# Batch 5's q and k loads between two parts of batch 4's value loads, and its crossbar transfers one tile later, in an attention and feed-forward kernel

## The chip, the cores and the metric

The kernel runs on one core of a Trainium2 chip. The metric is the time of one execution on the device in microseconds (us), the median of several runs. A profiled execution gives, besides, a trace of every instruction on each engine: TensorE (PE, and PEld for its weight loads), VectorE (DVE), ScalarE (ACT), GpSimd (POOL), SyncE (SP). GpSimd and SyncE do little here but issue transfers, each in its own order, on two queues that the same 16 DMA engines serve.

## The reference

Two things are computed one after the other, and only the last result is stored.

```python
# attention, (batch, heads, seq, head_dim) = (8, 8, 576, 64)
scores = scale * np.matmul(q, k.transpose(0, 1, 3, 2))
rel = pos[:, None] - pos[None, :]
mask_plain = (rel >= 0) & (rel < window)                                  # window = 32, heads 0 to 3
mask_dil = (rel >= 0) & (rel < window * dilation) & (rel % dilation == 0)  # dilation = 4, heads 4 to 7
scores = np.where(masks[None, :, :, :], scores, -1000000000.0)
attn = softmax(scores);  attn_out = np.matmul(attn, v)
# feed-forward over the 8 * 576 = 4608 tokens, d_model 512, d_ff 2048
h = np.maximum(x @ w_in, 0.0)
out = (h * h @ w_out).astype(np.float32)
```

Softmax is written short here. The inputs are float32 in memory; the loads turn them into bfloat16.

## The kernel before, in words

**Feed-forward.** The tokens are worked on in tiles: four of 256 and then seven of 512 (`ffn_groups`). Each tile is a list of groups. A group of layer one multiplies four k-slices of the weights with the attention result in `xT` (L888), ScalarE applies the relu and writes `h2T` (L901), VectorE squares it (L902). A group of layer two is four matmuls of L930; after four of them the sum is copied out by ScalarE (L936) and stored by SyncE (L857). A tile of 512 has 16 groups of layer one and 16 of layer two. All tiles together make one list of 288 groups, numbered from 0; a tile of 512 tokens has 32 (`G`). Tile 2 is groups 64 to 95, tile 3 groups 96 to 127, tile 4 groups 128 to 159.

**Attention in between.** Batches of attention are laid between the groups of tiles ahead of those that use their result. From batch 3 on (`NATURAL`) this goes by numbered steps: a list `steps` of (group, priority, batch, code), sorted, and taken off after each group. The codes are
- `R`, `K`, `Q` (`arrange`, L471 to L482): VectorE copies transposed q and k from the buffer `xx` to where the matmuls want them (`qT`, `kbd`). `R` takes the ends of each sequence, and `R00` begins with the second part of q and of k.
- `V` (`quadrants`, L617): a visit of TensorE, which computes scores of some pairs of heads and the weighted sums of others. A pair is two heads; each batch has four, 0 to 3.
- `E` (L654, L656, L663): ScalarE takes the exponentials of the scores, VectorE multiplies them by the mask, and for pairs 0 and 1 adds two sums.
- `L`, `X` (L630 to L645): the normalisation, by ScalarE and then VectorE, into `xT`.

For batch b a base `t = G * (b - 1)` fixes the groups: 96 for batch 4, 128 for batch 5. Batch 4 has a visit after group 111 that takes the weighted sum of its pair 0, and one after group 119 that takes scores of batch 5's pairs 2 and 0. Batches from `PAIRED` = 5 on copy `K` and `Q` for pair 0 and pair 1 at separate times.

**Transfers.** `load_qk` (L171) loads one part of q and of k of a batch on GpSimd's queue to a staging buffer, `qb` and `kb` (three of each, chosen by `STAGE`). Part 0 is 64 rows, part 1 is 80 rows, 256 elements of each head in a row. `load_v_rows` loads v on the same queue: with `d` the rows for the dilated heads and two blocks (L444, L449, eight transfers), with `0` and `1` the plain heads of that pair in sixteen-row pieces (L457, eight transfers each). A GpSimd transfer is issued only when the one eight places before it has landed. `cross_all` issues four crossbar transfers of a batch on SyncE's queue (L238, `DMA_TRANSPOSE`): k and q of part 0, then k and q of part 1, from the staging buffer to `xx[b % 2]`. They share SyncE's queue with the stores, in the order of the program.

**What sets the order.** Everything is issued in the order in which the program runs: the loop at L1128 goes through the groups, and after each group runs the codes that `PROGRAM` has at that place (its `|` separates groups), then the steps that are due. `Lb:q0...` and `Lb:q1...` are q and k loads of batch b, part 0 or 1; `Lb:V` with letters are its value loads; `Lb:x` its crossbar transfers. In `PROGRAM` batch 5 has its loads at groups 76 and 77, the values of batch 4 follow at 78, `L5:x` comes at 84, batch 6's loads at 93 and 94, and batch 5's values at 95. The later batches have theirs by `LOAD_V`, `CROSS` and `LOAD_QK` (L1055 to L1057). An engine takes an instruction only after the one before it, so the group at which something stands fixes its place in the queue and not the time at which it runs.

Of the kernel before, what the change touches and what calls it, by code (L numbers as in the profile page):

```python
# [26 lines left out]
    "| | | | | | | | | m n | | | | | | 1q1 1q3 | 1q2f 1k2f | 1k1a 1v3 | 1a2 | 1v2 1k0a 1q0v | 1o2 | 1a0 1a1 | 1k3 "  # L27
    "1o0 1o1f | 1a3 1Q0 | 1K0 1o3 | 1Q1 1K1 | 1Q2 | 1b0 | | 1Q3 1K2 L2:vwp L3:q00123 L3:q10123 L2:vwdr | L2:x | | "
    "2q0 | | 2k0 1V2 | 1b2 1p0 | 1b1 1V3 1K3 | L3:x | 1p2 1p1f | 2a0 1b3 | 2k1l 2b0 2o0 1p3f 2k1h | 2q1 | | 2p0 "
    "L3:Vd0 L4:q00123 L4:q10123 L3:V1 2a1 | 2b1 | | 2o1 | | | 2p1f | | | | L4:x | | | | | | | | | | | | | | | | "  # L30
    "L5:q10123 | L5:q00123 | L4:V | | | | | | L5:x | | | | | | | | | L6:q00123 | L6:q10123 | L5:V"
)


# [29 lines left out]
def kernel(  # L64
# [11 lines left out]
    B, H, S, D = q.shape  # L76
# [20 lines left out]
    PAIRED = 5  # L97
# [339 lines left out]
    def load_v_rows(b: int, which="d01"):  # L437


        if "d" in which:  # L440
            vds[b] = vd_pool.tile([P, NE // 2, 2, RES * D], bf16, name="vd")
            for hl, rows in enumerate(sides):
                for e in range(NE // 2):
                    nc.gpsimd.dma_start(  # L444
                        vds[b][rows, e, :, :],
                        v[b, H // 2 + 2 * e + hl, 0:512, :].rearrange("(m p r) d -> p m (r d)", p=64, r=RES),
                    )
                for i in (0, 8):
                    nc.gpsimd.dma_start(  # L449
                        v_rows[b % 2][rows, NE // 2 :, i, :],  # L450
                        v[b, H // 2 + hl : H : 2, 64 * i : 64 * i + 64, :].rearrange("h p d -> p h d"),
                    )
        for e in (int(x) for x in which if x != "d"):
            for hl in range(2):
                p0 = sides[hl ^ crossed(b, e)].start
                for r in range(RES):
                    nc.gpsimd.dma_start(  # L457
                        v_rows[b % 2][p0 + 16 * r : p0 + 16 * r + 16, e, :, :],
                        v[b, 2 * e + hl, :, :].rearrange("(i m r) d -> r m i d", r=RES, m=16)[r],
                    )  # L460
# [591 lines left out]
    G = 2 * NF  # L1052
# [1 line left out]

    LOAD_V = {b: G * (b - 2) for b in range(6, B)}  # L1055
    CROSS = {b: G * (b - 1) - 48 for b in range(6, B)}
    LOAD_QK = {b: G * (b - 3) - 10 for b in range(7, B)}  # L1057
    groups, steps = [], []
    for tk0, nt in [(NT // 2 * t, NT // 2) for t in range(4)] + [(NT * t, NT) for t in range(2, NTILES)]:
        groups += ffn_groups(tk0, nt)  # L1060
# [8 lines left out]
    for b in range(NATURAL, B):  # L1069
        t = G * (b - 1)  # L1070
        early = b == NATURAL
        def visit(at, scs, pvs):
            steps.append((at, 2, b, "V0" + "/".join(",".join(f"{x}{y}" for x, y in z) for z in (scs, pvs))))

        def expo(e, *at):
            steps.extend((y, 1, b, f"E{e}{x}") for x, y in enumerate(at))

        def norm(e, at):
            steps.extend([(at, 3, b, f"L{e}"), (at + 1, 0, b, f"X{e}")])

        after = b + 1 < B
        if b < PAIRED:
            start = 59 if early else t - 8
            second = t + (7 if early else 5)
            x = 3 if early else 0
            if early:
                visit(start, [(b, 2)], [(XB, 2), (XB, 3)])
                for e in (2, 3):
                    steps.extend([(start + e - 2, 3, XB, f"L{e}"), (start + e - 1, 0, XB, f"X{e}")])
            expo(2, *((start + 4, start + 7) if early else (start + 7, start + 9)))  # L1090
            visit(second, [(b, x)], [(b, 2)])
            norm(2, second)
            expo(x, second + 3, second + 5)
        if early:
            visit(t + 17, [(b, 0), (b, 1)], [(b, 3)])
            expo(0, t + 18, t + 18)
            expo(1, t + 18, t + 18)
            norm(3, t + 18)
            visit(t + 24, [(b + 1, 2)], [(b, 0), (b, 1)])
            norm(0, t + 24)  # L1100
            norm(1, t + 25)
        else:
            visit(t + 15, [(b, 3), (b, 1)], [(b, 0), (b, 2)][: 1 + (b >= PAIRED)])
            steps.extend((t + 15, 3, b, f"E1{x}") for x in range(2))
            if b >= PAIRED:
                norm(2, t + 15)
            expo(3, t + 16, t + 16)
            norm(0, t + 17)
            visit(t + 23, [(b + 1, 2), (b + 1, 0)] if after else [], [(b, 1), (b, 3)])
            if after:  # L1110
                steps.extend((t + 23, 3, b + 1, f"E0{x}") for x in range(2))
                steps.extend((t + 27 + 2 * x, 1, b + 1, f"E2{x}") for x in range(2))
            norm(3, t + 23)
            norm(1, t + 24)
        at = t - 14 if b < PAIRED else t - 26
        for x, code in enumerate(("R00", "R01", "R10", "R11")):
            steps.append(((57, 57, 54, 55)[x] if early else at + x, 1, b, code))
        for x, code in enumerate(("K00", "K01", "K10", "K11", "Q00", "Q01", "Q10", "Q11")):
            if b < PAIRED:
                steps.append((t + x if early else t - 6 + x, 1, b, code))  # L1120
            else:
                steps.append((t - 23 + x - max(x - 4, 0) // 2, 1, b, code + "0"))
                steps.append((t - 8 + x, 1, b, code + "1"))
    steps.sort(key=lambda x: x[:2])
    program = [x.split() for x in PROGRAM.split("|")]
# [2 lines left out]
    for g, group in enumerate(groups):  # L1128
        for b in [x for x in CROSS if CROSS[x] == g]:
            cross_all(b)  # L1130
        for b in [x for x in LOAD_V if LOAD_V[x] == g]:
            load_v_rows(b)
        for b in [x for x in LOAD_QK if LOAD_QK[x] == g]:
            for part in range(2):
# [36 lines left out]
```

## Time and profile before

| | us |
|---|---|
| median of three runs | 302.16 |
| the three runs | 301.69, 302.16, 302.79 |
| the profiled execution | 301.41 |
| its span, from first to last instruction | 299.6 |

| queue | packets | MB | share of 16 engines |
|---|---|---|---|
| GpSimd's (software) | 49280 | 18.43 | 56.0% |
| SyncE's (hardware) | 33120 | 16.18 | 25.9% |

The granted TensorE clock was 1.000 over the span. The profile's page gives, for each engine, its busy time; a row of 40 slices with the busy share in tenths; the chain of work that ended last, followed back from the end; and the groups of instructions by source line. The trace can be asked for more: instructions in order of time (start, length, engine, line, output and input, and in brackets the idle time before it with what ended that), who waited for whom, and for a stretch of time what each DMA queue moved (packets, MB, share) and how long transfers took from issue to landing. The tiles can be placed by the chain: tile 2's layer one starts at 88.57 us, its layer two at 103.15, tile 3's layer one at 119.05, its layer two at 135.11, tile 4's layer one at 150.02.

### The profile page before, as it was taken

How to read it: one execution, taken by the hardware profiler on the slowest of the kernel's cores; microseconds unless marked ns; L12 is line 12 of the kernel's file. 1: busy time of each engine (PE TensorE's matmuls, PEld its weight loads, DVE VectorE, ACT ScalarE, POOL GpSimd, SP SyncE). 2: the span in 40 equal slices, each digit the busy share in tenths (PEclk: the TensorE clock that was granted, in tenths of full speed). 3: DMA queues.
4: the chain of work that ended last, by engine and by line, in shares of the span. 5: the costliest groups of instructions: out<-in, count | busy, mean ns of one | idle time of the engine just before them, and what ended most of it. 6: DMA issues, size and time to landing. Idle time of an engine off the chain costs nothing.

```text
span 299.6 us, 7596 instructions
## 1 busy us (share of the span) xinstructions
PE 289.8 (97%) x3016; PEld 168.2 (56%) x3045; DVE 165.9 (55%) x495; ACT 193.7 (65%) x405; POOL 130.5 (44%) x210
## 2 busy tenths in 40 slices
PE   8889999999999999999999999999999999999994
PEld 3579756968855455554455455545555455445443
DVE  2675556998858654696748574856455235004300
ACT  7787658859967765786667666767666566126411
POOL 8589872585884538849838389000000000000000
PEclk9999999999999999999999999999999999999999
DMA  7999999999999999999994997012101200121022
GB/s 111 200 169 214 206 153 226 186 161 199 187 121 192 158 192 162 190 149 145 184 213 30 132 187 80 4 29 70 48 0 27 83 35 0 37 71 35 0 72 70
DMA packets 83123, 35.42 MB, mean 118 GB/s; under 512 B 52624, under 2 KB 78480, under 8 KB 83088
## 3 DMA queue, kind: packets, MB, share of 16 engines
q0 software_dynamic: 49280, 18.43, 56.0%
q1 hardware_dynamic: 33120, 16.18, 25.9%
q8 instruction: 24, 0.39, 0.5%
q10 hardware_dynamic: 688, 0.33, 0.5%
q14 instruction: 11, 0.09, 0.1%
HBM read 37.40 MB, written 9.44 MB: 156 GB/s over the span
## 4 chain that ended last, share of the span: by engine, by line
PE 90%; DMA 5%; POOL 1%; issue 1%; ACT 1%; DVE 0%; ACTq 0%; POOLq 0%
PE pf L930 41%; PE pf L888 41%; DMA w_in<-in_moe_w_in_dram 3%; DMA kb<-in_k_dram 2%; PE po L617 2%; PE pa L258 1%; PE pf L617 1%; PE pa L617 1%; PE pd L617 1%; POOL qb L171 1%; PE pa L332 1%; PE po L395 1%; PE pd L397 0%; POOL kb L171 0%; POOL vbd L219 0%
## 5 line engine op out<-in xcount | busy, mean ns | idle before, releaser
L888 PE MATMUL pf<-xT,w_in 128*128 128x512 bf16 (+1 forms) x697 | 128.3, 340 | 1.9 <-DMA w_in<-in_moe_w_in_dram 1.5
L930 PE MATMUL pf<-w_out_sb,h2T 128*128 128x512 bf16 (+2 forms) x570 | 127.4, 373 | 1.5 <-issue 0.6
L888 PEld LDWEIGHTS <-w_in 128*128 128x128 bf16 x704 | 77.7, 113 | 47.9 <-DMA w_in<-in_moe_w_in_dram 1.6
L901 ACT ACTIVATE h2T<-pf 128x512 bf16<-128x512 f32 x144 | 83.7, 599 | 30.0 <-PE pf L888 29.7
L902 DVE TENSOR_TENSOR h2T<-h2T 128x512 bf16<-128x512 bf16 x144 | 60.4, 424 | 60.9 <-ACT h2T L901 58.8
L930 PEld LDWEIGHTS <-h2T 128*128 128x128 bf16 x592 | 55.4, 98 | 61.1
L936 ACT COPY osb<-pf 128x512 f32<-128x512 f32 (+1 forms) x36 | 20.7, 574 | 52.6 <-PE pf L930 49.5
L457 POOL DMA_DIRECT2D vbd<-in_v_dram x80 | 43.9, 558 | 7.8 <-DMA vbd<-in_v_dram 2.9
L444 POOL DMA_DIRECT2D vd<-in_v_dram x20 | 12.1, 612 | 14.9 <-PE pf L617 6.1
L449 POOL DMA_DIRECT2D vbd<-in_v_dram x20 | 11.9, 606 | 12.1 <-DMA qb<-in_q_dram 5.4
L640 ACT ACTIVATE rec<-rec 128x576 f32<-128x576 f32 x22 | 15.0, 683 | 0.6
L192 POOL DMA_DIRECT2D vbd<-in_v_dram x16 | 10.9, 686 | 9.9 <-DMA kb<-in_k_dram 3.6
L654 ACT ACTIVATE pt<-pa 128x384 bf16<-128x384 f32 (+1 forms) x26 | 11.8, 497 | 4.5 <-DVE xT L645 2.7
L171 POOL DMA_DIRECT2D qb<-in_q_dram x18 | 13.2, 736 | 1.5 <-POOLq L1155 0.8
L643 DVE TENSOR_TENSOR xT<-po,rec 128x512 bf16<-128x512 f32 x13 | 9.0, 692 | 8.3 <-ACT rec L640 8.0
L171 POOL DMA_DIRECT2D kb<-in_k_dram x18 | 13.1, 730 | 0.7 <-DMA kb<-in_k_dram 0.7
L656 DVE TENSOR_TENSOR pt<-pt,mask_n 128x448 bf16<-128x448 bf16 (+1 forms) x20 | 7.1, 372 | 9.9 <-ACT pt L654 9.8
L656 DVE TENSOR_TENSOR pt<-pt,mask_f 128x384 bf16<-128x384 bf16 x24 | 8.2, 354 | 5.8 <-ACT pt L654 5.7
L471 DVE COPY qT<-xx 64x576 bf16<-64x576 bf16 (+1 forms) x32 | 11.1, 346 | 0.7
L643 DVE TENSOR_TENSOR xT<-pf,rec 128x512 bf16<-128x512 f32 x9 | 6.2, 691 | 7.4 <-ACT rec L640 7.3
L617 PEld LDWEIGHTS <-vbd 64*64 64x64 bf16 x248 | 6.8, 107 | 3.8 <-issue 2.9
L473 DVE COPY kbd<-xx 64x320 bf16<-64x320 bf16 (+3 forms) x32 | 8.4, 261 | 0.7
(138 smaller groups left out, 314.4 us busy)
## 6 DMA issues: line engine op xcount, KB each, us to landing
qb<-in_q_dram POOLq DMA_DIRECT2D x7, 320.0 KB, 7.8
kb<-in_k_dram POOLq DMA_DIRECT2D x7, 320.0 KB, 9.3
vd<-in_v_dram POOLq DMA_DIRECT2D x32, 64.0 KB, 7.0
w_in<-in_moe_w_in_dram POOLq DMA_DIRECT2D x4, 512.0 KB, 7.8
w_out_sb<-in_moe_w_out_dram POOLq DMA_DIRECT2D x4, 512.0 KB, 12.2
out_dram<-osb SPq DMA_DIRECT2D x16, 128.0 KB, 5.9
qb<-in_q_dram POOLq DMA_DIRECT2D x7, 256.0 KB, 6.8
kb<-in_k_dram POOLq DMA_DIRECT2D x7, 256.0 KB, 8.5
```

The source lines that it names most:

```text
L171: nc.gpsimd.dma_start(t[0:n, part, hs, :], src[b, hs, t0 : t0 + RES * n, :].rearrange("h (p r) d -> p h (r d)", r=RES))
L444: nc.gpsimd.dma_start(vds[b][rows, e, :, :], v[b, H // 2 + 2 * e + hl, 0:512, :].rearrange("(m p r) d -> p m (r d)", p=64, r=RES),)
L457: nc.gpsimd.dma_start(v_rows[b % 2][p0 + 16 * r : p0 + 16 * r + 16, e, :, :], v[b, 2 * e + hl, :, :].rearrange("(i m r) d -> r m i d", r=R ...
L617: nc.tensor.matmul(out, lhs, rhs, start=begin, stop=True, skip_group_check=True)
L640: nc.scalar.activation(rec[:, :], rec[:, :], ACT.Exp, scale=-1.0)
L643: nc.vector.tensor_tensor(out=tok[:, :, 16:M], in0=byr(o[:, :]), in1=byr(rec[:, 0:512]), op=ALU.mult)
L656: nc.vector.tensor_tensor(out=pt, in0=pt, in1=mask, op=ALU.mult)
L888: nc.tensor.matmul(to, w_in_sb[piece][:, kt, c0 : c0 + 509 : 4], rhs, start=(kt == kts[0] and x == 0), stop=(kt == kts[-1] and x == per - ...
L901: nc.scalar.activation(hv, acc[u][:, :].rearrange("p (x n) -> p x n", x=per), ACT.Relu)
L902: nc.vector.tensor_tensor(out=hv, in0=hv, in1=hv, op=ALU.mult)
L930: nc.tensor.matmul(cur[m][:, c0:c1], h2[:, f, P * m : P * m + P], w_out_sb[:, f, c0:c1], start=(f == 0), stop=(f == NF - 1),)
L936: (nc.vector.tensor_copy if last and part == 1 else nc.scalar.copy)(osb[:, c0:c1], cur[m][:, c0:c1])
```

## The change

Four edits, all in the order of work; no instruction is added or removed.

```diff
@@ PROGRAM
-    "L3:Vd0 L4:q00123 L4:q10123 L3:V1 2a1 | 2b1 | | 2o1 | | | 2p1f | | | | L4:x | | | | | | | | | | | | | | | | "
-    "L5:q10123 | L5:q00123 | L4:V | | | | | | L5:x | | | | | | | | | L6:q00123 | L6:q10123 | L5:V"
+    "L3:Vd0 L4:q00123 L4:q10123 L3:V1 2a1 | 2b1 | | 2o1 | | | 2p1f | | | | L4:x | | | | | | | | | | | | | | | | | "
+    "| L4:Vd0 L5:q00123 L5:q10123 L4:V1 L6:q00123 L6:q10123 | | | | | | | | | | | | | | | | | L5:V | | L5:x"
@@
-    LOAD_QK = {b: G * (b - 3) - 10 for b in range(7, B)}
+    LOAD_QK = {b: G * (b - 3) - 2 for b in range(7, B)}
@@
-        at = t - 14 if b < PAIRED else t - 26
+        at = t - (14, 23, 26)[(b >= PAIRED) + (b > PAIRED)]
@@
-                steps.append((t - 23 + x - max(x - 4, 0) // 2, 1, b, code + "0"))
+                steps.append((t - (20 if b == PAIRED else 23) + x - max(x - 4, 0) // 2, 1, b, code + "0"))
```

On GpSimd's queue, batch 4's values for the dilated heads and the first plain pair now stand ahead of batch 5's q and k, whose part 0 comes before part 1 where it was the other way round; batch 4's second plain pair follows, then batch 6's q and k, then batch 5's values as before. All of these but batch 5's values are handed out after group 78. On SyncE's queue, batch 5's four crossbar transfers move from group 84 to group 97, behind five stores of tile 2. On VectorE, batch 5's `R` copies move from groups 102 to 105 to groups 105 to 108, and the `K` and `Q` copies for its pair 0 from groups 105 to 111 to groups 108 to 114. Batch 7's q and k are handed out at group 126 and not 118, which leaves them at the same place on GpSimd's queue. The instructions of TensorE and ScalarE keep their order.

## The prediction

> **What bounds the kernel now.** I read the shares by engine first, then the chain that ended last, then TensorE's own waits, then the order of work on SyncE's queue and VectorE around the change. The first three say that TensorE sets the time:
>
> ```profile
> PE 289.8 (97%) x3016; PEld 168.2 (56%) x3045; DVE 165.9 (55%) x495; ACT 193.7 (65%) x405; POOL 130.5 (44%) x210
> ...
> DMA  7999999999999999999994997012101200121022
> ...
> PE 90%; DMA 5%; POOL 1%; issue 1%; ACT 1%; DVE 0%; ACTq 0%; POOLq 0%
> ```
>
> TensorE is busy for 289.8 of 299.6 us; of the 9.8 us left, its longest waits by name are 1.5 us for the first weights and 1.1 us at the start, both before 21 us. In the windows 100 to 125 and 125 to 150 us I find 0.3 us of idle and none. So in the stretch that the change touches (95 to 145 us) there is nothing to win on TensorE in this execution, and the change can only matter by putting a wait where none is. The DMA row shows where such a wait could come from: the 16 DMA engines are at nine tenths or more from 7.5 us to 157 us. Any transfer that is moved later there has to share with what is running then.
>
> Now the transfers that are moved. SyncE's queue, with the start and length of each issue:
>
> ```profile
> 89.03 1.37 SPq L238 DMA_TRANSPOSE xx<-kb  x1
> ...
> 97.00 1.29 SPq L238 DMA_TRANSPOSE xx<-qb  x1
> 98.39 11.84 SPq L857 DMA_DIRECT2D out_dram<-osb  x5
> 110.42 1.28 SPq L238 DMA_TRANSPOSE xx<-kb  x1
> 111.81 1.82 SPq L238 DMA_TRANSPOSE xx<-qb  x1
> 113.74 2.27 SPq L238 DMA_TRANSPOSE xx<-kb  x1
> 116.10 2.30 SPq L238 DMA_TRANSPOSE xx<-qb  x1
> 118.50 2.87 SPq L857 DMA_DIRECT2D out_dram<-osb  x5
> 134.55 1.25 SPq L238 DMA_TRANSPOSE xx<-kb  x1
> ```
>
> The sets at 89, 110 and 134 us are those of batches 4, 5 and 6. The one at 110.42 is batch 5's; its last transfer landed 5.2 us after 116.10, at 121.3. VectorE reads it first at 128.90, so it had 7.6 us in hand:
>
> ```profile
> 109.74 0.19 DVE L479 COPY kbd<-xx 64x128 bf16<-64x128 bf16 x1 [1.47 <-DMA xx<-qb]
> ...
> 127.80 0.69 DVE L643 TENSOR_TENSOR xT<-po,rec 128x512 bf16<-128x512 f32 x1
> ...
> 128.90 0.19 DVE L479 COPY kbd<-xx 64x128 bf16<-64x128 bf16 x1
> ...
> 132.33 0.41 DVE L902 TENSOR_TENSOR h2T<-h2T 128x512 bf16<-128x512 bf16 x1
> 132.66 0.34 DVE L656 TENSOR_TENSOR pt<-pt,mask_n 128x384 bf16<-128x384 bf16 x1
> 133.04 0.34 DVE L663 TENSOR_TENSOR kbd<-pt 128x128 bf16<-128x128 bf16 x2
> ...
> 137.22 0.31 DVE L471 COPY qT<-xx 64x576 bf16<-64x576 bf16 x1
> ```
>
> VectorE works without a gap from 127.80 to 140.24. What TensorE needs of it are two things: the masked scores of batch 4's pair 0 (done 133.38) for the visit at 133.85 (after layer-one group 111), and batch 5's rearranged q and k (done 137.53) for the visit at 141.75 (after group 119).
>
> **The change, part by part.** *Loads.* GpSimd's queue has the same instructions in another order. From 95.23 on, eight issues of L444 and L449 (some 0.61 each) and eight of L457 (0.56) now go before batch 5's four loads: 4.9 + 4.5 = 9.4 us, so these start at about 104.6 instead of 95.23. They took 7.1 to 12.4 us to land; four issues of 0.73 bring the last to 107, landing at 114 to 119. That is ahead of the transposes' new place (below), so by itself it costs 0. If the last landed at 121 or later, SyncE would wait by as much, added one for one to what follows. Batch 4's second half of L457 comes after them and is read only at 141.75: 0. Batch 6's loads, which began at 121.06 after all of this, now follow without batch 5's transposes beside them and start at some 113 to 118. Batch 7's loads (now handed out at group 126, before at 118) keep their place between batch 5's and 6's values on GpSimd's queue: 0.
>
> *Transposes.* Four issues on SyncE move behind five stores. The last two of these need the eviction of the fourth token block, 119.09 + 0.59 = 119.68; at 2.87/5 = 0.57 an issue the queue is free at 120.9. So 110.42 becomes 120.9, 10.5 us later, and of the 7.6 us in hand nothing is left unless VectorE's own move helps. The stores themselves go earlier (the first of the five at about 112 instead of 118.5): they free an output buffer that nobody waits for here, 0.
>
> *VectorE.* Its reads of the transposed data move three groups later. Now three squarings (L902, 0.43 each) and one mask (0.41) come before the first read: 128.87 + 1.70 = 130.6. That first read needs the fourth transfer of the set, because it takes the second part of q. Behind it on VectorE stand a squaring, the second mask and its two sums: 0.43 + (133.41 - 132.33 = 1.08) = 1.51 us. TensorE wants these at 133.85. So the last transfer may land at 133.85 - 1.51 = 132.3 at the latest; after that each us costs TensorE one us. The second need: from the first read to the end of the q copies VectorE had 11.34 us of work; without the four instructions that now go ahead, 9.64. With the landing at T, q is ready at T + 9.64, wanted at 141.75 plus whatever the first wait cost; at T = 134.2 that adds 0.2 us. The squarings are wanted later than both: in the new order the q copies come behind the sixteenth of them.
>
> *How long the set takes to land* is the disputed term. From first issue to last landing the six sets of this trace took 9.0 (batch 2), 13.3 (3), 20.7 (4), 10.9 (5), 12.5 (6) and 9.9 us (7). What tells them apart is what the other queue moved meanwhile; in the windows of batch 4's, 5's and 6's sets it was:
>
> ```profile
> q0 software_dynamic: 4899, 1.95, 85.9%
> ...
> q0 software_dynamic: 2838, 0.43, 52.7%
> ...
> q0 software_dynamic: 2907, 0.41, 50.9%
> ```
>
> Packets, MB and share; the transposes' own queue had 4990, 5017 and 4893 packets. So 0.42 MB beside it means 11.7 us, 1.95 MB means 20.7: 5.9 us for each MB. At 120.9 I expect about half of batch 6's loads still running (0.3 of 0.59 MB), then batch 5's value rows (0.13 MB of L444 and most of L457's 0.29): 0.7 MB, 11.7 + 0.28 x 5.9 = 13.3 us, batch 3's own figure. Landing at 134.2. Ends: 9.0 us (129.9, no wait) and 20.7 us (141.6, a wait of 9.3 us). I take 13.3 because the neighbours will be more than batch 5's and 6's sets had and less than half of batch 4's.
>
> The Trainium skill ("DMA: Bandwidth & Descriptors", section "Latency and other measured facts") gives transposes an effective 261 GB/s. A set reads 2 x 8 x 576 x 64 bf16 = 1.18 MB, an estimate of 4.5 us by that page: it would be there before 130.6 and the whole sum would be 0. No set in this trace came under 9.0 us, so I go by the sets.
>
> **Sum.** 134.2 + 1.51 - 133.85 = 1.9, plus 0.2 at the second visit: 2.1 us. The profiled execution took 301.41 us (span 299.6 and 1.8 around it), which gives 303.5. Its time lies below all three timed runs (301.69 to 302.79, median 302.16); the median plus 2.1 is 304.3. Some of that 0.75 may be a wait that the change removes (next part), so I forecast 303.8, some 0.1 below the middle of 303.5 and 304.3.
>
> **Rivals.** *Faster: the set of batch 4 comes early enough.* Its last transfer took 12.7 us because batch 5's loads ran beside it; VectorE waited 1.47 us for it (first line of the VectorE view), and its last copy ended at 112.56, while TensorE reached scores with that data at 112.54 to 112.68. There is 0.1 us in hand. A run where that transfer lands later pays in full, and the three timed runs lie 0.28 to 1.38 above the profiled one. With batch 4's values in place of batch 5's loads there, less is moved beside that set and this goes away. If all of the 0.75 is this, and batch 5's set lands by 132.3, the time is 302.16 - 0.75 = 301.4; it is faster by over 0.3% if the wait it removes exceeds 0.91 us, and 1.38 would give 300.8. Against it: the profiled execution has no such wait. 0.17.
>
> *No change.* Batch 5's set takes 11.4 us or less (as batches 2, 5 and 7 did) and everything is hidden: 302.2, between 301.4 and 303.0. For it: half of the sets. Against: they had quieter neighbours. 0.28.
>
> *Much slower.* Batch 6's loads are later than I think, and the set runs beside them whole, as batch 4's did: 20.7 us, 9.3 us of wait, 311.5. Against: batch 6's loads have no transposes beside them from 110 to 121. 0.07.
>
> *My forecast,* a wait of 0.9 to 4 us before the visits at 133.85 and 141.75: 0.48.
>
> **How the numbers follow.** Within 0.3% (0.9 us) is what a measurement of this kernel can't tell from no change. Slower: 0.48 + 0.07 = 0.55; the same 0.28; faster 0.17. The forecast's own range is 303.1 to 306.2. For 8 in 10 I go down to 301.2, which takes in no change and the likelier part of the faster case, and leave out the 311.5.
>
> **What would show it.** In the new profile: batch 5's four transposes at about 121 on SyncE; VectorE's L479 with some 3 to 4 us of idle behind a transposed tile, near 134; TensorE waiting for VectorE at the visits near 134 and 142 us, by about 2 us together; all later stages shifted by that and nothing else. Batch 4's last transposed transfer landing before 108 would support the faster case's premise. I am wrong if that L479 has no idle, or if the transposes start after 123 because batch 5's loads landed late, or if the visit's wait is for another engine.

## The result, and the profile after

The changed kernel takes 318.03 us, the median of six runs (315.39 to 319.41); before, six runs gave 302.02 (300.91 to 302.79). The ratio is 1.0521, with a 95% interval of 1.0465 to 1.0577: about 16 us slower. The forecast was 303.8, within 301.2 to 306.2. The direction was right and the size was not. (In two experiments below, the second and the seventh, the profiled execution was one of the chip's slower ones, so there the timed ratios count and the profile is read only for who waited.)

The profiled execution took 315.77 us, its span 314.0 against 299.6. From the page of the changed kernel, the engines, the busy tenths of TensorE, the granted clock and the chain:

```profile
PE 293.0 (93%) x3016; PEld 169.6 (54%) x3045; DVE 166.2 (53%) x495; ACT 193.4 (62%) x405; POOL 129.5 (41%) x210
...
PE   8889999999999999908987999999999999999995
...
PEclk9999999999999999975999999999999999999999
...
PE 74%; DMA 14%; SPq 4%; DVE 2%; ACT 2%; issue 2%; POOL 1%; ACTq 0%; POOLq 0%
```

TensorE has one empty slice, the eighteenth (133 to 141 us), and another that is only part full soon after. In the first and in the slice behind it the clock row drops to 7 and 5. DMA and SyncE's queue, which had 5% and nothing of the chain, now have 14% and 4%. Whom TensorE waited for (total, times, longest):

```profile
PE po L617 <- DVE pt L656: 8.1, 1, 8.1
PE pf L888 <- ACT osb L936: 3.2, 1, 3.2
```

With 293.0 - 289.8 = 3.2 us more of busy time, for the same 3016 matmuls, that is 8.1 + 3.2 + 3.2 = 14.5, against 14.4 us of longer span. So all of the profiled execution's loss is found; the medians lie 16.0 us apart, and the 1.6 us more were not traced. The three terms are the first wait, the second wait and the clock.

The first wait, in the order of VectorE's instructions and then of SyncE's queue:

```profile
129.78 0.42 DVE L902 TENSOR_TENSOR h2T<-h2T 128x512 bf16<-128x512 bf16 x1
140.89 0.19 DVE L479 COPY kbd<-xx 64x128 bf16<-64x128 bf16 x1 [10.69 <-DMA xx<-qb]
...
141.47 0.34 DVE L656 TENSOR_TENSOR pt<-pt,mask_n 128x384 bf16<-128x384 bf16 x1
141.85 0.34 DVE L663 TENSOR_TENSOR kbd<-pt 128x128 bf16<-128x128 bf16 x2
```

```profile
120.55 1.32 SPq L238 DMA_TRANSPOSE xx<-kb  x1
121.97 3.37 SPq L238 DMA_TRANSPOSE xx<-qb  x1
125.44 6.76 SPq L238 DMA_TRANSPOSE xx<-kb  x1
132.32 4.92 SPq L238 DMA_TRANSPOSE xx<-qb  x1
143.30 2.07 SPq L238 DMA_TRANSPOSE xx<-kb  x1
145.49 1.24 SPq L238 DMA_TRANSPOSE xx<-qb  x1
146.84 2.25 SPq L238 DMA_TRANSPOSE xx<-kb  x1
149.18 7.90 SPq L238 DMA_TRANSPOSE xx<-qb  x1
157.18 10.37 SPq L857 DMA_DIRECT2D out_dram<-osb  x8
```

Batch 5's set begins at 120.55, as worked out, and its last transfer lands at 140.89: 20.3 us, where before it took 10.9. VectorE sits 10.69 us before the copy that needs it, the mask behind that copy is done at 141.8, and TensorE, which wanted it at 133.75, goes on at 141.87. Batch 6's set follows at 143.30 and its last transfer lands 15.9 us after 149.18, at 165.1: 21.8 us. Tile 3's stores, of which the first block was ready soon after 149.9, stand behind it until 157.18. ScalarE then lacks an output buffer, and TensorE an accumulator (ScalarE's instructions around there):

```profile
157.55 0.58 ACT L936 COPY osb<-pf 128x512 f32<-128x512 f32 x1 [0.72 <-PE pf L930]
158.03 0.88 ACT L654 ACTIVATE pt<-pa 128x384 bf16<-128x384 f32 x2
166.15 0.58 ACT L936 COPY osb<-pf 128x512 f32<-128x512 f32 x1 [7.24 <-DMA out_dram<-osb]
```

Why the set was slow: GpSimd's queue, and the software queue's packets, MB and share between 120.55 and 140.9.

```profile
113.24 0.54 POOL L457 DMA_DIRECT2D vbd<-in_v_dram  x1 [0.53 <-DMA kb<-in_k_dram]
117.03 0.55 POOL L457 DMA_DIRECT2D vbd<-in_v_dram  x1 [3.25 <-DMA qb<-in_q_dram]
119.45 0.53 POOL L457 DMA_DIRECT2D vbd<-in_v_dram  x1 [1.88 <-DMA kb<-in_k_dram]
119.97 0.70 POOL L171 DMA_DIRECT2D qb<-in_q_dram  x1
```

```profile
q0 software_dynamic: 4446, 1.62, 80.9%
```

Three of the last value transfers each wait for one of batch 5's loads, eight places before them; so batch 6's loads begin only at 119.97. They run whole beside the set. Before, the first of them stood here, 1.1 us later, as batch 5's set was landing (121.3):

```profile
121.06 0.70 POOL L171 DMA_DIRECT2D qb<-in_q_dram  x1
```

### The profile page after: what moved, and what is told of

Read it like the earlier page. It is cut to its first block, busy times and chain, and to the rows that moved or that the text cites. A ratio compares the mean times of both kernels' runs of the same rounds, so it can differ in the third digit from the quotient of the medians.

```text
span 314.0 us, 7595 instructions
## 1 busy us (share of the span) xinstructions
PE 293.0 (93%) x3016; PEld 169.6 (54%) x3045; DVE 166.2 (53%) x495; ACT 193.4 (62%) x405; POOL 129.5 (41%) x210
## 4 chain that ended last, share of the span: by engine, by line
PE 74%; DMA 14%; SPq 4%; DVE 2%; ACT 2%; issue 2%; POOL 1%; ACTq 0%; POOLq 0%
PE pf L930 34%; PE pf L888 33%; DMA out_dram<-osb 4%; SPq L238 3%; DMA xx<-qb 3%; DMA vd<-in_v_dram 3%; DMA vbd<-in_v_dram 3%; DMA kb<-in_k_dram 2%; PE po L617 1%; PE pa L258 1%; DVE h2T L902 1%; PE pf L617 1%; PE pa L617 1%; PE pd L617 1%; POOL kb L171 1%
## 5 line engine op out<-in xcount | busy, mean ns | idle before, releaser
L930 PE MATMUL pf<-w_out_sb,h2T 128*128 128x512 bf16 (+2 forms) x570 | 129.2, 377 | 1.7 <-issue 0.9
L930 PEld LDWEIGHTS <-h2T 128*128 128x128 bf16 x592 | 55.9, 99 | 62.6 <-issue 2.5
L457 POOL DMA_DIRECT2D vbd<-in_v_dram x80 | 43.5, 557 | 12.4 <-DMA qb<-in_q_dram 4.8
L444 POOL DMA_DIRECT2D vd<-in_v_dram x20 | 12.1, 619 | 24.5 <-PE pf L617 19.0
L617 PE MATMUL po<-pt,vbd 64*64 64x96 bf16 (+2 forms) x170 | 8.5, 208 | 8.1 <-DVE pt L656 8.1
L192 POOL DMA_DIRECT2D vbd<-in_v_dram x16 | 10.9, 690 | 10.8 <-DMA kb<-in_k_dram 4.6
L654 ACT ACTIVATE pt<-pf 128x448 bf16<-128x448 f32 (+1 forms) x16 | 7.4, 521 | 9.4 <-PE pf L617 9.4
L617 PEld LDWEIGHTS <-mk 64*64 64x64 bf16 x284 | 7.0, 109 | 8.1 <-issue 8.1
## 6 DMA issues: line engine op xcount, KB each, us to landing
w_out_sb<-in_moe_w_out_dram POOLq DMA_DIRECT2D x4, 512.0 KB, 12.3
```

What stands on the lines that cost most here:

```text
L457: nc.gpsimd.dma_start(v_rows[b % 2][p0 + 16 * r : p0 + 16 * r + 16, e, :, :], v[b, 2 * e + hl, :, :].rearrange("(i m r) d -> r m i d", r=R ...
L617: nc.tensor.matmul(out, lhs, rhs, start=begin, stop=True, skip_group_check=True)
L654: nc.scalar.activation(pt, sp[b, e][g][:, 0:n], ACT.Exp, scale=SCALE)
L930: nc.tensor.matmul(cur[m][:, c0:c1], h2[:, f, P * m : P * m + P], w_out_sb[:, f, c0:c1], start=(f == 0), stop=(f == NF - 1),)
```

## The experiments

Eleven kernels were run. Ratios are to the kernel before, measured beside each.

**1. Crossbar back.** From the changed kernel:

```diff
-    "| L4:Vd0 L5:q00123 L5:q10123 L4:V1 L6:q00123 L6:q10123 (17 bars) L5:V | | L5:x"
+    "| L4:Vd0 L5:q00123 L5:q10123 L4:V1 L6:q00123 L6:q10123 | | | | | | L5:x (11 bars) L5:V"
```

> The changed kernel with batch 5's four crossbar transfers back at group 84; the loads' new order and VectorE's new groups stay. Theory N (the set's landing is set by what GpSimd's queue moves beside it, and at 120.5 us that is batch 6's loads): the set starts as batch 5's loads land (111 to 119 us), ends near 126, no wait of VectorE for a transposed tile, TensorE as before: 302 us, within 1 us of before. Rival O (the new order of the loads itself makes data late, wherever the crossbar stands): above 305 us. Rival F (the new order relieves batch 4's set and this is worth something): 0.5 to 1 us below before.

Ratio 1.002 (0.998 to 1.006). The time is that of before, so the loads' new order (with VectorE's) costs nothing that can be told, and the relief of batch 4's set gains nothing that can be told. My detail was wrong: the set began at 116.50 and its last transfer, issued at 122.55, took 13.4 us. It landed near 136, 19.5 us after it began, and the profiled execution had 3.0 us of wait at the first visit. It too ran beside batch 6's loads.

**2. Loads as before, crossbar and VectorE's copies as changed.**

```diff
-    "L5:q10123 | L5:q00123 | L4:V | | | | | | L5:x | ... | L6:q00123 | L6:q10123 | L5:V"
+    "L5:q10123 | L5:q00123 | L4:V | ... | L6:q00123 | L6:q10123 | L5:V | | L5:x"
```

> The kernel before with two parts of the change: batch 5's crossbar transfers at group 97 and VectorE's copies at the new groups; all loads in their old order. N: batch 6's loads are issued at 121 us there, beside the set at 120.5, so it lands after some 20 us, near 141; VectorE waits about 10 us, TensorE about 8 at the first visit; 312 to 319 us. O: 302 us, because the loads are in their old order.

317.17 us (314.46 to 323.49), ratio 1.0425 (1.032 to 1.053). The loss is there with the old loads, so it belongs to the crossbar's place (experiment 4 has VectorE's copies alone). In its profile VectorE waits for the set at the same copy, and TensorE goes on at the first visit at 150.31, just after the mask behind that copy, done at 150.26. The profile puts that wait down to a value transfer; the order of times speaks for the mask.

**3. Batch 6's loads behind batch 5's values.** From the changed kernel:

```diff
-    ... L4:V1 L6:q00123 L6:q10123 | ... | L5:V | | L5:x
+    ... L4:V1 | ... | L5:V L6:q00123 L6:q10123 | | L5:x
```

> The changed kernel with batch 6's q and k loads handed out behind batch 5's values (after group 95) and not ahead of them. N: beside the set at 120.5 are now only batch 5's values, 0.42 MB with what is around them, so it lands after 11 to 13 us, at 131.5 to 133.5; TensorE's wait at the first visit is under 1.5 us. The second wait, for an output buffer behind batch 6's set, can stay: 302 to 306 us. O: 315 to 319 us as changed.

The first half came as expected. VectorE's first read of batch 5's set, and what the software queue moved in the 12 us beside that set:

```profile
133.13 0.20 DVE L479 COPY kbd<-xx 64x128 bf16<-64x128 bf16 x1 [2.38 <-DMA xx<-qb]
```

```profile
q0 software_dynamic: 2938, 0.44, 52.1%
```

The set took 12.0 us (121.09 to 133.1), and TensorE had no wait for the mask. The second half did not: the ratio is 1.0365 (1.028 to 1.045), because batch 6's own set, from 138.64, now had q and k loads beside it, took 19.9 us and held the stores. TensorE waited 6.2 us there.

**4. VectorE's copies alone,** from the kernel before:

```diff
-        at = t - 14 if b < PAIRED else t - 26
+        at = t - (14, 23, 26)[(b >= PAIRED) + (b > PAIRED)]
...
-                steps.append((t - 23 + x - max(x - 4, 0) // 2, 1, b, code + "0"))
+                steps.append((t - (20 if b == PAIRED else 23) + x - max(x - 4, 0) // 2, 1, b, code + "0"))
```

> The kernel before with VectorE's copies at the new groups and nothing else. N: the set lands at 121 us as before, no wait: 302 us, within 0.5. Rival V (VectorE's new order by itself delays the q and k copies for the visit near 142 us): 303 us or more.

Ratio 1.0006 (0.996 to 1.005): nothing, as expected.

**5. Both sets clear.** Experiment 3 with batch 7's loads behind batch 6's values:

```diff
-    LOAD_QK = {b: G * (b - 3) - 2 for b in range(7, B)}
+    LOAD_QK = {b: G * (b - 3) for b in range(7, B)}
```

> The third experiment once more, with batch 7's q and k loads as well behind the values before them (batch 6's). Theory N (a crossbar set takes 11 to 13 us beside value loads and some 20 us beside q and k loads, and all of the loss follows from that): batch 5's set lands near 133 as in the third experiment, batch 6's set, from about 138, now takes 11 to 13 us too, no wait of ScalarE for an output buffer at tile 3's end, TensorE's waits back to those of before; ratio to before 0.995 to 1.010. If a crossbar set at group 97 costs something else: 1.02 or more.

Ratio 1.0131 (1.008 to 1.018), just over what I expected. Batch 5's set took 12.1 us, batch 6's 12.3 (140.62 to 152.9). ScalarE still waited 5.3 us for an output buffer, TensorE 1.3 for ScalarE.

**6. Only batch 7's loads put behind,** the same edit in the changed kernel.

> The changed kernel with batch 7's q and k loads behind batch 6's values, batch 6's loads left as changed. N: TensorE's wait of about 8 us at the first visit stays, since batch 5's set still has batch 6's loads beside it; the wait of 3 us or more for an output buffer goes. 309 to 314 us, ratio 1.025 to 1.04. If the second wait is only the echo of the first: no change from 315 to 319.

313.98 us, ratio 1.0397 (1.034 to 1.045). The first wait is alone now (TensorE's instructions with a wait before them):

```profile
143.25 0.24 PE L617 MATMUL po<-pt,vbd 64*64 64x96 bf16 x1 [8.56 <-DVE pt L656]
```

Batch 5's set took 20.8 us, batch 6's 10.6, and ScalarE's wait in tile 3 is gone. The second wait is a thing of its own.

**7. Tile 3's stores on ScalarE's queue,** in the changed kernel:

```diff
-            nc.sync.dma_start(out[...], osb[x : x + n, c0:c1])
+            queue = nc.scalar if 3 * NT <= pos < 4 * NT else nc.sync
+            queue.dma_start(out[...], osb[x : x + n, c0:c1])
```

> The changed kernel with tile 3's eight stores issued by ScalarE and not by SyncE, so that they aren't queued behind batch 6's crossbar set. Theory Q (the second wait is the queue: the stores stand behind a slow set): batch 6's set stays at 20 us or more, ScalarE's wait for an output buffer in tile 3 goes, 309 to 314 us. Rival S (the stores land late because the DMA engines are busy): the wait stays above 2 us, 315 to 319 us.

Not settled by this: 318.46 us (314.87 to 324.44), ratio 1.0501 (1.041 to 1.059). The wait for the buffer went, but ScalarE, issuing a store, itself waited, and TensorE waited for ScalarE. The edit moved the wait and did not remove it.

**8. VectorE's copies for batch 5 later still,** in the changed kernel:

```diff
-        at = t - (14, 23, 26)[(b >= PAIRED) + (b > PAIRED)]
+        at = t - (14, 16, 26)[(b >= PAIRED) + (b > PAIRED)]
...
-  (t - (20 if b == PAIRED else 23) + ...
+  (t - (15 if b == PAIRED else 23) + ...
```

> The changed kernel with VectorE's R copies for batch 5 moved on from groups 105 to 108 to groups 112 to 115, and its K and Q copies for pair 0 from 108 to 114 to 113 to 119. Theory H (the wait of 8 us is one of order on VectorE: the mask that TensorE needs stands behind a copy that waits for the crossbar): no wait at the first visit near 134, the set still lands near 141, and TensorE waits at the second visit instead, by 141 + 5 of copies - 142 = 4 us; 309 to 315 us. If TensorE needed the transposed data at the first visit: 315 to 319 us.

310.65 us, ratio 1.0295 (1.023 to 1.037). TensorE's waits between 100 and 190 us:

```profile
144.84 0.53 PE L617 MATMUL po<-pt,vbd 64*64 64x96 bf16 x2 [2.85 <-DVE xT L643]
...
147.46 0.28 PE L617 MATMUL pf<-qT,kbd 64*64 64x96 bf16 x1 [2.09 <-DVE qT L471]
148.12 0.53 PE L617 MATMUL pf<-qT,kbd 64*64 64x96 bf16 x16 [0.37 <-DVE qT L471]
```

No wait at the first visit, although the set landed at 142.98, later than as changed. TensorE waits at the second, 5.3 us in all where I expected 4. So of the 8.1 us a good third was VectorE's order: the mask stood behind a copy that had to wait. The second wait is gone as well: batch 6's set began at 138.13, not 143.30, and took 12.0 us.

**9. Batch 6's loads beside batch 5's set at its old place.** Experiment 1 with the two parts swapped:

```diff
-    ... L4:V1 L6:q00123 L6:q10123 | | | | | | L5:x
+    ... L6:q00123 L6:q10123 L4:V1 | | | | | | L5:x
```

> The first experiment (crossbar at group 84) with batch 6's q and k loads ahead of the second part of batch 4's values, so that they run beside batch 5's set at its old place. Theory N: the set, begun at 113 to 117, takes 17 to 21 us and not 11 to 13, and lands at 131 to 136; TensorE waits up to 4 us at the first visit: 303 to 308 us, ratio 1.005 to 1.02. If what slowed the set was the hour at which it ran (the stores, batch 5's values) and not batch 6's loads: the set takes 11 to 13 us, ratio below 1.005.

VectorE's first read of the set, which began at 112.88:

```profile
133.48 0.18 DVE L479 COPY kbd<-xx 64x128 bf16<-64x128 bf16 x1 [3.35 <-DMA xx<-qb]
```

20.6 us, with 1.96 MB on the other queue. The hour makes no difference, the neighbours do. And it cost hardly anything, 0.9 us of TensorE in the profile and a ratio of 1.0039 (0.9995 to 1.008), because it began 8 us earlier. A slow set and a late one are both needed for the loss.

**10. Two stores ahead of batch 6's set,** in the changed kernel:

```diff
-    CROSS = {b: G * (b - 1) - 48 for b in range(6, B)}
+    CROSS = {b: G * (b - 1) - (40 if b == 6 else 48) for b in range(6, B)}
```

> The changed kernel with batch 6's crossbar set handed out at group 120 and not 112, so that the stores of tile 3's first two blocks stand ahead of it on SyncE's queue. Theory Q (the second wait is queue order: those stores stand behind a set that takes 14 to 22 us): ScalarE's wait for an output buffer in tile 3 goes, the first wait of about 8 us stays; 309 to 314 us, ratio 1.025 to 1.04. Batch 6's set may land late enough to cost something at its own reader. Rival S (the DMA engines are busy, and the stores land late wherever they stand): the wait for the buffer stays above 2 us, ratio 1.045 or more.

310.35 us, ratio 1.0305 (1.025 to 1.036). SyncE's queue, and what TensorE still waited for:

```profile
147.79 4.63 SPq L857 DMA_DIRECT2D out_dram<-osb  x4
152.59 1.77 SPq L238 DMA_TRANSPOSE xx<-kb  x1
```

```profile
PE po L617 <- DVE pt L656: 7.0, 1, 7.0
```

The stores go ahead, the wait for the buffer is gone, the first wait stays. The second wait was the order on SyncE's queue; this is what experiment 7 could not show.

**11. All clear.** Its predecessor is experiment 5, here with the first block's stores ahead of batch 6's set (the last edit with 44 for 40).

> The kernel with both sets clear of q and k loads, and the stores of tile 3's first block ahead of batch 6's set on SyncE's queue. Its predecessor kept 1.3% over before, with a wait of 5.3 us of ScalarE for an output buffer in the profiled execution. Theory Q (that rest is the stores behind the set): the wait goes and the ratio is 0.996 to 1.006. If something else in the late crossbar costs it: 1.01 or more. Theory N for batch 5's set: it takes 11 to 13 us from about 120.5.

303.15 us, ratio 1.0024 (0.9988 to 1.0059). Batch 5's set is still at 121.16, landing at 133.35, and TensorE has no wait from it. With the neighbours and the queue mended, the late crossbar costs nothing that can be told; it brings nothing either. No version beat the kernel before.

## Why the prediction was wrong

**What held.** TensorE as the bound and no gain on it: every version that lost no time came to 1.000 to 1.004. The set's start (120.9 worked out, 120.55 measured). VectorE's order: its first read of the set was worked out for 130.6 and it was ready for it at 130.2. The price of lateness: the wait should be the landing less 132.3, for 140.89 that is 8.6, and it was 8.1. The set's duration as a matter of what the other queue moves: the line of 5.9 us for each MB gives 11.7 + 1.2 x 5.9 = 18.8 for the 1.62 MB that there were; measured 20.3. That is an agreement at the line's upper end only. Between the ends the line fails: batch 3's set before had 1.01 MB beside it and took 13.3 us where the line has 15.2, batch 4's as changed had 0.87 MB and took 11.5 where it has 14.4. The lower end of the range, 9.0 us, was batch 2's set, and in this kernel `cross` moves only half of the heads of that batch (`XB`); the shortest whole set before was batch 7's, 9.9 us.

**The step that failed** is the estimate of neighbours, "about half of batch 6's loads still running (0.3 of 0.59 MB)", which made 0.7 MB, 13.3 us and a landing at 134.2. In the run they began at 119.97, so that none of them was over when the set began at 120.55: 1.62 MB beside it and not 0.7, 20.3 us and not 13.3, landing at 140.89. I let them start at 113 to 118, by adding up issue times. I had written that a load lands 7.1 to 12.4 us after its issue, and in the section on the kernel that an issue waits for the eighth transfer before it; put together, the last value transfers must wait for batch 5's last load, which landed at 119.45 (I had allowed 114 to 119). That puts batch 6's loads at 119.97, exactly beside the set; they had begun at 121.06 before, so the new order moved them by 1.1 us. The amount was wrong too: 0.59 MB is q or k of a batch alone (320 and 256 KB), and both are 1.18 MB. With half of that the sum would have been 1.0 MB, 15.1 us and a wait of 3.7 us, still less than half of what came. The rival "much slower", 311.5, was this mechanism with nearly its right price (9.3 us of wait, against 8.1), and had 0.07; I argued against it with "batch 6's loads have no transposes beside them from 110 to 121", which is true and beside the point.

**What the sum lacked.** I wrote "all later stages shifted by that and nothing else". Two more terms came. The second wait, 3.2 us: batch 6's set, pushed back by the first wait into batch 7's loads, held tile 3's stores (experiments 6 and 10 remove it and leave the first). I had followed SyncE's queue for batch 5's set and its stores, and not for the next set. And 3.2 us of slower matmuls, of which the last section places 2.9 behind the first wait.

**The second visit** added nothing measured, where 0.2 was expected. **Batch 7's loads** I set at 0 because their place on GpSimd's queue was the same; their place was the same, but the queue was ahead of where it had been relative to batch 6's set. Before, they began 8.8 us after that set (143.36 and 134.55), now 2.5 us after it (145.77 and 143.30), and ran beside most of it (experiment 6).

**The faster rival** was right in its premise and worth nothing: batch 4's set landed by 104, VectorE's wait of 1.47 us for it went, and experiment 1 has a ratio of 1.002.

## What to carry to other kernels

When transfers are reordered on one queue, place each by its own limits (its buffer, and a wait for the transfer so many places before it), not by adding up issue times; then lay the other queue's transfers against it and price each by what runs beside it. Where a transfer is late, look at what stands behind its reader and behind its issuer in the same queue: here a mask that didn't need it, and stores that didn't either, carried the loss to TensorE. And a bound engine that is made to wait may run slower for a while after, which belongs in the sum.

## What the runs showed of the hardware

A set of four crossbar transfers moves 1.18 MB and took 10.6 to 12.5 us where it had mostly value loads beside it (batch 5's and 6's before, batch 5's in experiments 3, 5 and 11, batch 6's in 5 and 6) and 19.3 to 22.1 us where it had q and k loads (both as changed, batch 5's in 1, 6, 8, 9 and 10, batch 6's in 3), whatever the hour. Batch 6's in experiments 1, 4, 8, 9 and 10 took 11.3 to 12.9 us, with 0.35 to 0.81 MB on the other queue. In between stood batch 6's in experiment 11, with 15.0 us and part of its own loads still running at its start. Among the slow sets the time does not rise with the amount (22.1 us beside 1.57 MB, 19.9 beside 2.07); what it is in q and k loads that slows a set, no run separates. The two groups come to some 100 and 58 GB/s, against the 261 GB/s of the page cited in the prediction.

The clock after a wait: stretches of the changed kernel (us, busy time and count for each engine, granted TensorE clock, DMA share, GB/s).

```profile
133.00:142.00 9.00, 0.88 (x7) 0.40 (x5) 1.07 (x6) 1.12 (x2) 5.96 (x12) 0.75 1.30 160
142.00:146.00 4.00, 3.78 (x77) 2.39 (x76) 3.74 (x15) 2.22 (x6) 4.00 (x8) 0.50 0.90 63
146.00:150.00 4.00, 4.00 (x16) 1.59 (x15) 3.81 (x13) 2.14 (x5) 2.59 (x4) 0.78 1.25 155
...
163.00:167.00 4.00, 0.77 (x4) 0.30 (x3) 0.00 (x0) 0.85 (x2) 2.85 (x6) 1.00 1.36 254
167.00:172.00 5.00, 5.00 (x25) 2.65 (x24) 3.36 (x10) 4.09 (x8) 3.38 (x7) 1.00 0.67 83
```

After the wait of 8.1 us the clock stood at 0.50 and came back at about 148. The matmuls of L930 between the two visits, before (first line) and as changed (the other two):

```profile
134.66 7.08 PE L930 MATMUL pf<-w_out_sb,h2T 128*128 128x512 bf16 x31
...
143.65 0.61 PE L930 MATMUL pf<-w_out_sb,h2T 128*128 128x512 bf16 x1
144.48 8.27 PE L930 MATMUL pf<-w_out_sb,h2T 128*128 128x512 bf16 x30 [0.22 <-issue]
```

The 31 took 9.10 us (143.65 to 152.75) where they took 7.08 before, and from the first visit to tile 4's first matmul it was 18.93 us (141.87 to 160.80) where it had been 16.07 (133.78 to 149.85), 2.9 us more. After the wait of 3.2 us, at 163.6 to 166.8, the clock stayed at 1.00. The Trainium skill ("TensorE: Matmul & The Clock Gate", section "What's actually happening") has the clock fall to half after an idle window of some 3.4 us; both waits agree with that.

The length of the wait alone does not decide it, as experiment 8 shows. The windows in which the clock fell and came back, as changed (first two lines) and in experiment 8:

```profile
137.50:137.75 0.25, 0.00 (x0) 0.00 (x0) 0.00 (x0) 0.00 (x0) 0.25 (x1) 0.56 1.33 184
147.75:148.00 0.25, 0.25 (x2) 0.10 (x1) 0.25 (x3) 0.00 (x0) 0.25 (x2) 0.96 1.03 164
...
144.25:144.50 0.25, 0.00 (x0) 0.00 (x0) 0.25 (x1) 0.00 (x0) 0.25 (x1) 0.69 1.33 193
151.00:151.25 0.25, 0.24 (x1) 0.15 (x1) 0.00 (x0) 0.22 (x2) 0.25 (x1) 0.65 0.72 34
```

As changed it fell 3.8 us after the matmuls stopped (133.75). In experiment 8 they stopped at 141.99, and it fell at about 144.35, after 2.4 us, in a wait of only 2.85. From fall to return it was 10.2 us as changed and in experiment 6, and 6.8 in experiments 3, 8 and 10, three and two times 3.4. That looks as if the clock changed only at steps of 3.4 us, so that it also counts how a wait lies among them; no run was made to test this. What can be said of the price: the wait of 8.1 us cost some 11 (8.1 + 2.9), the one of 3.2 cost 3.2, and the 5.3 us of waits in experiment 8 cost 7.8 (5.3 and 292.3 - 289.8 = 2.5 of longer busy time; its span is 307.4 against 299.6).
